# Folding the next batch on GpSimd, row copies on VectorE, and other steps for the transforms

## The chip, the cores and the metric

One Trainium2 chip, one of its cores. The metric is the device time of one execution in microseconds (us). The engines are named as the trace names them: PE is TensorE (matmuls; PEld its weight loads), DVE is VectorE, ACT is ScalarE, POOL is GpSimd, SP is the engine that issues most DMAs.

## The reference

```python
X = np.fft.fft(x, axis=1)                 # x: 8 batches, 3072 positions, 256 features
X = np.fft.fft(X, axis=2).real            # 24576 tokens of 256
h = x @ w_in                              # 256 -> 2048
g = h * (1.0 / (1.0 + np.exp(-1.702 * h)))
x = g @ w_out                             # 2048 -> 256
# second MoE layer: tokens with x @ w_skip > 0 go to the expert of the largest gate logit
y[mask] = gate_w[mask, None] * (np.maximum(xc[mask] @ w1[e], 0.0) @ w2[e])
out[do_compute] = xc + y
```

All of it is in float32. The kernel gets that accuracy from matmuls with operands split into a high and a low part (`yh`, `yl`, `gh`, `gl`, `sh`, `sl`, `woh`, `wol`): the low part is the value minus its rounded high part.

## The kernel before

Phase 1 makes the Fourier transform and the first MLP and routes tokens to experts; phase 2 runs the eight experts over the routed rows. The change touches phase 1 alone.

The transform over the sequence is cut by symmetry. **Folds** first add and subtract mirrored rows of a batch, which arrive as six `raw` tiles: `pq` (512 columns), `eo` (two of 256), `ub` (two of 128), `va` (two of 128; for the middle pair of tiles, t = 1, four of 64 partitions), and once for each pair of tiles `tm` (256 and twice 128). ACT rounds `tm` and `va` to `sh`, POOL subtracts to get `sl`. Each batch then has eight **transforms** (`piece_mm`: 9 matmuls into the one PSUM bank with the tag "misc"), four even and four odd, whose results DVE, ACT and POOL turn into `yh` and `yl`.

Phase 1 then walks over 16 half-batches `hb` of 24 steps, 384 steps `g` in all. A block `gb` is 512 tokens and 8 steps; the 2048 hidden units are taken 256 a step. In step g:

- `hstep(g)`: 12 matmuls (L850) to two `pt` tiles (three PSUM buffers), then on DVE `pp` twice (L854) and `h` twice (L856, L857);
- `ystep(g - 2)`: 24 matmuls (L881) from `gh` and `gl` of two steps before into four PSUM banks y0 to y3. In a block's last step the order is bank by bank, in the others all `gh` parts come ahead of all `gl` parts;
- `gelu(g)`: ACT makes `gh` (L864) and `h` (L865), POOL makes `gl = h - gh` (L866). `h` and `gl` have two buffers, `gh` three;
- two steps after a block's last step `finish` copies the four banks to `rows` (L887: y0, y1 on DVE, y2, y3 on ACT). The next `ystep` starts a new block in these banks and needs them free;
- last, the **side list** of the step: functions that `plan` has put there by step number (transforms, their evacuations, folds, loads), and the route that `finish` appends. A block that is copied in step n (n = 1, 9, 17 of a half-batch, from the block before) has `a1` in step n + 1 (on DVE: the row ids at L891, then `route1`, six small operations L779 to L784 that end in `roh`, and the store of the rows), `a2` in n + 2 (PE: small matmuls of `roh`, L793 and L795, into the "misc" bank), `a3` in n + 3 (DVE, L805 to L809), and one scatter (POOL, an indirect DMA, L813) in each of n + 4 to n + 7.

Every engine takes its instructions in the order in which the program emits them; waits between engines are semaphores. So the step numbers in `plan` decide what stands ahead of what. Odd transforms of a batch run in its even half-batch, even transforms of the next batch in its odd one. The folds of the next batch also begin in the even half-batch and reach into the odd one (steps 24 and up are steps 0 and up of the odd one). The folds of batch 1, in half-batch 0, have a list of slots of their own.

Of the kernel before, what the change touches and what calls it, by code (L numbers as in the profile page):

```python
# [18 lines left out]
ALU = mybir.AluOpType  # L19
# [15 lines left out]
TB = 512  # L35
NBLK = HC // PB
NSTEP = NF // 2
RW = 266
NW = 264
# [125 lines left out]
class Phase1:  # L165
# [53 lines left out]
        e2.tensor_sub(eo[:, 1], pq[:, 0], pq[:, 1])  # L219
        return eo  # L220

    def fold_ub(self, ab, eo, ub):
        v = self.nc.vector
        v.tensor_add(ub[:, 0, ab], eo[:, 0, 0], eo[:, 0, 1])
        v.tensor_sub(ub[:, 1, ab], eo[:, 1, 0], eo[:, 1, 1])

    def fold_va(self, t, ab, eo, va):
        v = self.nc.vector
        for kind, op in ((0, v.tensor_sub), (1, v.tensor_add)):
            x, y = eo[:, kind, 0], eo[:, kind, 1]  # L230
            at_a = ab == kind
            if t == 1:
                if at_a:
                    op(va[0:64, kind, 0, 1], x[0:64], y[0:64])
                    op(va[64:128, kind, 1, 1], x[64:128], y[64:128])
                else:
                    op(va[64:128, kind, 0, 1], x[0:64], y[0:64])
                    op(va[0:64, kind, 1, 1], x[64:128], y[64:128])
            else:
                op(va[:, kind, t // 2, 0 if at_a else 2], x, y)  # L240

    def fold_tm(self, ub):
        v = self.nc.vector
        tm = self.fb.tile([P, 4, P], F32, tag="tm", bufs=1, name="tm")
        v.tensor_add(tm[:, 0::3], ub[:, :, 0], ub[:, :, 1])
        v.tensor_sub(tm[:, 2], ub[:, 0, 0], ub[:, 0, 1])
        v.tensor_sub(tm[:, 1], ub[:, 1, 0], ub[:, 1, 1])
        return tm

    def fold_even(self, t, ub, sh, sl, le):  # L250
        tm = self.fold_tm(ub)
        shv, slv = sh[:, :, t], sl[:, :, t]
        self.nc.scalar.copy(shv, tm)
        le.tensor_sub(slv, tm, shv)
# [83 lines left out]
    def startup(self):  # L338
# [156 lines left out]
        def fold(j):  # L495
            if j % 2 == 0:
                q["ub"] = self.new_ub()
            eo = q["eo", j] = st.tile([P, 2, 2, P], F32, name=f"eo{j}")
            self.fold_ub(j % 2, self.fold_eo(self.fold_pq(raws[j], v), v, eo), q["ub"])

        def tmsh(t):
            q["tm"] = self.fold_tm(q["ub"])
            act.copy(sh[:, :, t], q["tm"])

        def slv(t):
# [136 lines left out]
                if (n or k == "c") and (n < 9 or k == "a"):  # L642
                    at(n, k, f, n)
        for j in range(6):
            at(j + 1, "d", lambda j=j: self.fold_va(j // 2, j % 2, q.pop(("eo", j)), va))
        at(3, "c", self.ahead_pad)
        for f, fe, p, n in ((piece, piece_ev, 2, 1), (piece, piece_ev, 3, 1), (nine, nine_ev, 2, 3), (nine, nine_ev, 4, 5), (nine, nine_ev, 5, 6)):
            at(n, "d", f, p)
# [7 lines left out]
    def plan(self, hb):  # L656
        nc = self.nc
        b, odd = hb // 2, hb % 2
        g0 = hb * NBLK * NSTEP
        last = hb == 2 * self.nb - 1  # L660
        if last:
            return
        add = lambda s, f: self.side[g0 + s].append(f)
        le = nc.gpsimd
        st = {}
        if not odd:
            def prep():
                st["cm"] = self.cm if hb == 0 else self.cmn
                st["y"] = self.new_y(hb + 1)
                self.y[hb + 1] = st["y"]  # L670
            add(9 if hb == 0 else 0, prep)
            if hb == 0:
                for c in range(4):
                    add(7 + c, lambda c=c: self.split_odd(self.va, *self.s, c, le))
            def p0(p):
                sh, sl = self.s
                q = self.piece_mm(st["cm"][4 + p % 2], sh, sl, p, KC)
                st["q"] = q
            def e0(p):
                st["xp"] = self.evac_odd0(b, p, st["q"])  # L680
            def e1(p):
                self.evac_odd1(p, st["xp"], st["q"], *st["y"], le)
            for p, s in enumerate((10, 13, 15, 21) if hb == 0 else (1, 4, 6, 7)):
                add(s, lambda p=p: p0(p))
                add(s + 1, (lambda p=p: e0(p)) if p % 2 == 0 else (lambda p=p: e1(p)))
            if b + 1 < self.nb:
                def ld(i):
                    st["r", i] = self.load_raw(b + 1, i // 2, i % 2)

                def f1(i):  # L690
                    st["pq"] = self.fold_pq(st["r", i], nc.vector)
                    if i + 3 < 6:
                        ld(i + 3)

                def f2(i):
                    if i == 0:
                        self.va = self.new_va()
                    if i % 2 == 0:
                        st["ub"] = self.new_ub()
                    st["eo"] = self.fold_eo(st["pq"], nc.vector)  # L700

                def fa(i):
                    f1(i)
                    f2(i)

                def fu(i):
                    self.fold_ub(i % 2, st["eo"], st["ub"])

                def fv(i):
                    self.fold_va(i // 2, i % 2, st["eo"], self.va)  # L710

                def fr(i):
                    fu(i)
                    fv(i)

                def fe(t):
                    if t == 0:
                        self.sn = self.new_s()
                    self.fold_even(t, st["ub"], *self.sn, le)

                def nx():
                    self.s = self.sn
                    self.cmn = {0: self.load_c(0), 1: self.load_c(1)}

                if hb == 0:
                    seq = []
                    for t in range(3):
                        for i in (2 * t, 2 * t + 1):
                            seq += [lambda i=i: fa(i), lambda i=i: fr(i)]
                        seq.append(lambda t=t: fe(t))  # L730
                    slots = (13, 15, 19, 21, 23, 24, 27, 29, 30, 31, 32, 35, 37, 38, 39)
                    for i in range(3):
                        add(10 + i, lambda i=i: ld(i))
                    for s, f in zip(slots, seq):
                        add(s, f)
                else:
                    for i in range(3):
                        add(i, lambda i=i: ld(i))
                    for f, steps in ((f1, (3, 11, 14, 21, 24, 29)), (f2, (6, 13, 16, 21, 24, 29)), (fu, (6, 13, 16, 23, 27, 30)), (fv, (7, 14, 19, 22, 27, 30)), (fe, (15, 23, 31))):
                        for i, s in enumerate(steps):  # L740
                            add(s, lambda f=f, i=i: f(i))
                add(23, nx)
        else:
            def prep():
                st["cm"] = self.cmn
                st["y"] = self.new_y(hb + 1)
                self.y[hb + 1] = st["y"]
            add(0, prep)
            def p0(p):
                sh, sl = self.s  # L750
                st["q"] = self.piece_mm(st["cm"][p], sh, sl, p, CW if p == 0 else KC)
                if p < 2:
                    st["cm"][p + 2] = self.load_c(p + 2)
                else:
                    self.cmn2 = getattr(self, "cmn2", {}) if p == 3 else {}
                    self.cmn2[p + 2] = self.load_c(p + 2)
                    if p == 3:
                        self.cmn = self.cmn2
            def e0(p):
                self.evac_even(b + 1, p, st["q"], *st["y"], le)  # L760
            for p, s in enumerate((16, 18, 20, 22) if b == 0 else (10, 13, 15, 18)):
                add(s, lambda p=p: p0(p))
                add(s + 1, lambda p=p: e0(p))
            def sp(c):
                if c == 0:
                    self.s = self.new_s()
                self.split_odd(self.va, *self.s, c, le)
            for c in range(4):
                add(22 + c // 2 if b == 0 else 20 + c, lambda c=c: sp(c))
# [57 lines left out]
    def main(self):  # L827
# [10 lines left out]
        if True:  # L838
# [44 lines left out]
            def finish(gb, gnow):  # L883
                st = {}
                rows = self.rp.tile([P, 4, RW], F32, tag="rows", bufs=2, name="rows")
                for t in range(4):
                    (v.tensor_copy if t < 2 else nc.scalar.copy)(rows[:, t, :NW], ys[gb][t])  # L887
                del ys[gb]

                def a1():  # L890
                    v.scalar_tensor_tensor(rows[:, :, NW:], self.rid[:, 1], float(gb * TB), self.rid[:, 0], ALU.mult, ALU.add)  # L891
                    st["oh"] = self.route1(rows, 4)
                    nc.sync.dma_start(self.a["out"][gb * TB : (gb + 1) * TB].rearrange("(t p) d -> p t d", p=P), rows[:, :, :D])

# [505 lines left out]
```

## Time and profile before

| | us |
|---|---|
| median of 3 runs | 2405.22 (2400.37 to 2409.26) |
| the profiled execution | 2406.35 |
| its span, first to last instruction | 2404.2 |
| PE busy in the span | 2344.2 (98%) |
| DVE busy | 1682.4 (70%) |
| ACT busy | 1121.3 (47%) |
| POOL busy | 1396.3 (58%) |

The profiled execution lies 1.1 us above the median of the runs. Ends of matmuls are modelled, and a matmul is recorded for longer than the next one's distance from it, so a busy PE does not say that no time is lost: for that one compares how long steps take that hold the same work. The start of a step is the first L850 matmul of its `hstep`. A window cut from one such start to the next gives the length of a step.

### The profile page before, as it was taken

The page shows a single profiled execution, that of the slowest core. Times are in us where ns is not written, and L with a number is a line of the kernel's source. Part 1 is how long each engine was busy: PE and PEld are TensorE (multiplying, and loading weights), DVE is VectorE, ACT ScalarE, POOL GpSimd, SP SyncE. Part 2 cuts the span into 40 slices and gives each one's busy share as a digit, 9 for nine tenths or more (in the row PEclk, how much of TensorE's full clock was granted, in tenths as well). Part 3 has the DMA queues.
Part 4 walks back from the last instruction along what each step waited for, and adds up shares of the span by engine and source line. Part 5 has one row for each costly group of instructions (what it writes and reads, how often), then busy time and mean ns, then how long its engine had stood idle before and what let it go on. Part 6 is the DMA issues. An engine that isn't in the chain of part 4 may idle for free. (4 is left out here: it accounts for less than half of the span.)

```text
span 2404.2 us, 50497 instructions
## 1 busy us (share of the span) xinstructions
PE 2344.2 (98%) x19222; PEld 2308.6 (96%) x19222; DVE 1682.4 (70%) x3429; ACT 1121.3 (47%) x1451; POOL 1396.3 (58%) x868
## 2 busy tenths in 40 slices
PE   6999999999999999999999999999999999999999
PEld 4899999999999999999999999999999999999999
DVE  7679679768966896698679768965756445555543
ACT  5644545455454454455444455445544333433332
POOL 3567667676677676767767767667666312323211
PEclk8999999999999999999999999999999999999999
DMA  7312312231131123112312221130101312323111
GB/s 261 117 34 78 125 44 69 66 102 37 66 99 63 46 70 113 47 38 85 116 34 79 73 87 48 60 105 21 62 20 33 108 44 84 116 84 119 36 45 39
DMA packets 91449, 178.82 MB, mean 74 GB/s; under 512 B 10895, under 2 KB 66750, under 8 KB 85104
## 3 DMA queue, kind: packets, MB, share of 16 engines
q1 hardware_dynamic: 69488, 96.12, 12.9%
q0 software_dynamic: 20448, 77.87, 9.3%
q8 instruction: 132, 2.16, 0.4%
q10 hardware_dynamic: 1312, 2.10, 0.3%
q14 instruction: 69, 0.57, 0.1%
HBM read 126.21 MB, written 66.59 MB: 80 GB/s over the span
## 5 line engine op out<-in xcount | busy, mean ns | idle before, releaser
L866 POOL TENSOR_TENSOR gl<-h,gh 128x1024 fp32r<-128x1024 f32 x384 | 922.7, 2403 | 519.0 <-ACT h L865 429.4
L864 ACT ACTIVATE gh<-h 128x1024 fp32r<-128x1024 f32 x384 | 407.5, 1061 | 854.4 <-DVE h L857 711.7
L881 PE MATMUL py<-woh,gh 128*128 128x264 f32 x3072 | 771.0, 285 | 9.6 <-ACT rows L887 9.0
L881 PE MATMUL py<-wol,gh 128*128 128x264 f32 x3072 | 767.0, 283 | 0.0
L881 PEld LDWEIGHTS py<-woh,gh 128*128 128x128 f32 x3072 | 579.4, 189 | 14.2 <-ACT rows L887 13.6
L881 PEld LDWEIGHTS py<-wol,gh 128*128 128x128 f32 x3072 | 578.5, 188 | 0.0
L854 DVE SCALAR_TENSOR_TENSOR pp<-rb,w,pt 128x256 f32<-128x256 f32 x768 | 333.6, 475 | 297.1 <-PE pt L850 296.6
L881 PE MATMUL py<-woh,gl 128*128 128x264 f32 x3072 | 460.8, 284 | 0.9 <-POOL gl L866 0.9
L850 PE MATMUL pt<-yh,wch 128*128 128x256 f32 x1536 | 434.1, 283 | 4.4 <-DVE pp L854 2.8
L850 PE MATMUL pt<-yl,wch 128*128 128x256 f32 x1536 | 429.2, 279 | 0.5 <-POOL yl L300 0.5
L850 PE MATMUL pt<-yh,wcl 128*128 128x256 f32 x1536 | 428.5, 279 | 0.0
L865 ACT ACTIVATE h<-h 128x1024 f32<-128x1024 f32 x384 | 407.6, 1061 | 36.2 <-ACT gh L864 1.5
L881 PEld LDWEIGHTS py<-woh,gl 128*128 128x128 f32 x3072 | 410.0, 189 | 1.1 <-POOL gl L866 1.1
L856 DVE TENSOR_TENSOR h<-pp,pt 128x512 f32<-128x512 f32 x384 | 264.4, 689 | 55.9 <-POOL gl L866 4.6
L850 PEld LDWEIGHTS pt<-yh,wch 128*128 128x128 f32 x1536 | 290.5, 189 | 5.7 <-DVE pp L854 3.3
L850 PEld LDWEIGHTS pt<-yl,wch 128*128 128x128 f32 x1536 | 291.7, 190 | 1.0 <-POOL yl L300 0.7
L850 PEld LDWEIGHTS pt<-yh,wcl 128*128 128x128 f32 x1536 | 290.6, 189 | 0.0
L1281 POOL DMA_INDIRECT out<-ob,ix x82 | 80.3, 980 | 337.3 <-DVE ob L1295 335.1
L857 DVE TENSOR_TENSOR h<-pp,pt 128x512 f32<-128x512 f32 x384 | 261.3, 680 | 0.0
L813 POOL DMA_INDIRECT xs<-rows,rix x192 | 194.7, 1014 | 44.1 <-issue 25.0
L1267 PE MATMUL h<-xh,w1h 128*128 128x256 f32 x656 | 184.4, 281 | 5.6 <-PEq L1325 3.8
L1303 PE MATMUL po<-w2h,hh 128*128 128x256 f32 x656 | 188.6, 287 | 0.0
(221 smaller groups left out, 3493.9 us busy)
## 6 DMA issues: line engine op xcount, KB each, us to landing
cmat<-cm POOLq DMA_DIRECT2D x48, 1158.0 KB
raw<-raw SPq DMA_DIRECT2D x48, 512.0 KB
out<-rows SPq DMA_DIRECT2D x48, 512.0 KB
r<-w SPq DMA_DIRECT2D x14, 1024.0 KB
nx<-xs SPq DMA_DIRECT2D x33, 266.0 KB, 3.0
rb<-yd SPq DMA_DIRECT2D x48, 128.0 KB
wide<-w_in SPq DMA_DIRECT2D x8, 512.0 KB
wide<-w_out SPq DMA_DIRECT2D x8, 512.0 KB
```

The costliest lines, as they stand in the source:

```text
L813: i = self.nc.gpsimd.indirect_dma_start(self.xs, bass.IndirectOffsetOnAxis(ap=ix[:, t : t + 1], axis=0), rows[:, t], None, bounds_check=E ...
L850: nc.tensor.matmul(pt[z][:, i], lhsT=w_[:, z, f], rhs=x_[:, z, cols], start=n == 0, stop=n == 2)
L854: v.scalar_tensor_tensor(pp[:, i], r, self.w128[:, 2 * s + i : 2 * s + i + 1], pt[0][:, i], ALU.mult, ALU.add)
L856: v.tensor_add(h[:, :, 0], pp, pt[1])
L857: v.tensor_sub(h[:, :, 1], pp, pt[1])
L864: nc.scalar.activation(gh, hv, AF.Gelu_apprx_sigmoid)
L865: nc.scalar.activation(hv, hv, AF.Gelu_apprx_sigmoid)
L866: nc.gpsimd.tensor_sub(gl, hv, gh)
L881: nc.tensor.matmul(ys[gb][t], lhsT=x_[:, i, tk], rhs=w_[:, 2 * s + i], start=s == 0 and part is hi and n == 0, stop=ends and part is lo an ...
L1267: nc.tensor.matmul(h[:, z], lhsT=w_[:, k, f * P : (f + 1) * P], rhs=x_[:, k], start=i == 0, stop=i == 5)
L1281: d = self.nc.gpsimd.indirect_dma_start(self.out, bass.IndirectOffsetOnAxis(ap=ix, axis=0), ob, None, bounds_check=self.ntok - 1, oob_is_e ...
L1303: self.nc.tensor.matmul(po[t], lhsT=x_[:, f, t * P : (t + 1) * P], rhs=w_[:, f], start=f == 0 and n == 0, stop=f == 7 and n == 2)
```

## The change

1. The folds that start in the even half-batches 2 to 12 (six of the seven times that a next batch is folded inside the loop) run on POOL: `fold_pq`, `fold_eo`, `fold_ub`, `fold_tm` and `fold_va`, this one without t = 1, which stays on DVE. Half-batch 0 keeps its folds on DVE and its slots.
2. `fold_even` is split in `ft` (the `tm` fold) and `fc` (the copy on ACT and the subtraction on POOL), with steps of their own; all fold steps are new, and the first three raw loads are issued three steps earlier.
3. The row ids are written on POOL in `finish`: a memset of one column and an add, in place of one operation on DVE in `a1`.
4. All four row copies are on DVE.
5. Transforms: odd ones from steps 1, 4, 6, 7 to 1, 5, 7, 13; even ones from 10, 13, 15, 18 to 8, 13, 15, 17. Half-batches 0 and 1 keep theirs.

```diff
-            for p, s in enumerate((10, 13, 15, 21) if hb == 0 else (1, 4, 6, 7)):
+            for p, s in enumerate((10, 13, 15, 21) if hb == 0 else (1, 5, 7, 13)):
...
+                fo = nc.vector if hb == 0 else nc.gpsimd
...
-                    st["pq"] = self.fold_pq(st["r", i], nc.vector)
+                    st["pq"] = self.fold_pq(st["r", i], fo)
...
-                    st["eo"] = self.fold_eo(st["pq"], nc.vector)
+                    st["eo"] = self.fold_eo(st["pq"], fo)
...
-                    self.fold_ub(i % 2, st["eo"], st["ub"])
+                    self.fold_ub(i % 2, st["eo"], st["ub"], fo)
...
-                    self.fold_va(i // 2, i % 2, st["eo"], self.va)
+                    self.fold_va(i // 2, i % 2, st["eo"], self.va, nc.vector if i // 2 == 1 else fo)
...
-                def fe(t):
+                def ft(t):
+                    st["tm"] = self.fold_tm(st["ub"], fo)
+
+                def fc(t):
                     if t == 0:
                         self.sn = self.new_s()
-                    self.fold_even(t, st["ub"], *self.sn, le)
+                    self.split_even(t, st["tm"], *self.sn, le)
...
-                        add(i, lambda i=i: ld(i))
-                    for f, steps in ((f1, (3, 11, 14, 21, 24, 29)), (f2, (6, 13, 16, 21, 24, 29)), (fu, (6, 13, 16, 23, 27, 30)), (fv, (7, 14, 19, 22, 27, 30)), (fe, (15, 23, 31))):
+                        add(i - 3, lambda i=i: ld(i))
+                    for f, steps in ((f1, (1, 4, 9, 16, 22, 26)), (f2, (2, 5, 11, 17, 24, 27)), (fu, (3, 7, 12, 18, 25, 28)), (fv, (3, 8, 13, 19, 25, 28)), (ft, (10, 20, 29)), (fc, (15, 21, 30))):
...
-            for p, s in enumerate((16, 18, 20, 22) if b == 0 else (10, 13, 15, 18)):
+            for p, s in enumerate((16, 18, 20, 22) if b == 0 else (8, 13, 15, 17)):
...
+                nc.gpsimd.memset(rows[:, :, NW : NW + 1], 0.0)
+                nc.gpsimd.tensor_scalar_add(rows[:, :, RW - 1 :], self.rid[:, 0, :, 1:], float(gb * TB))
                 for t in range(4):
-                    (v.tensor_copy if t < 2 else nc.scalar.copy)(rows[:, t, :NW], ys[gb][t])
+                    v.tensor_copy(rows[:, t, :NW], ys[gb][t])
...
-                    v.scalar_tensor_tensor(rows[:, :, NW:], self.rid[:, 1], float(gb * TB), self.rid[:, 0], ALU.mult, ALU.add)
```

What this makes of the order on two engines, for half-batch 2. On DVE, from the `h` of step 17 to the first route operations of step 18, the order before was:

```order
L856 TENSOR_TENSOR h<-pp,pt 128x2x256
L857 TENSOR_TENSOR h<-pp,pt 128x2x256
L887 COPY rows<-py_4163 128x264
L887 COPY rows<-py_4164 128x264
L854 SCALAR_TENSOR_TENSOR pp<-rb,w_71,pt 128x256 x2
L856 TENSOR_TENSOR h<-pp,pt 128x2x256
L857 TENSOR_TENSOR h<-pp,pt 128x2x256
L891 SCALAR_TENSOR_TENSOR rows<-rid 128x4x2
L779 TENSOR_REDUCE rm<-rows 128x4
L780 TENSOR_TENSOR rq<-rows,rm 128x32
```

Now (the lines of the changed kernel are some five higher):

```order
L861 TENSOR_TENSOR h<-pp,pt 128x2x256
L862 TENSOR_TENSOR h<-pp,pt 128x2x256
L894 COPY rows<-py_4171 128x264
L894 COPY rows<-py_4172 128x264
L894 COPY rows<-py_4173 128x264
L894 COPY rows<-py_4174 128x264
L859 SCALAR_TENSOR_TENSOR pp<-rb,w_71,pt 128x256 x2
L861 TENSOR_TENSOR h<-pp,pt 128x2x256
L862 TENSOR_TENSOR h<-pp,pt 128x2x256
L784 TENSOR_REDUCE rm<-rows 128x4
L785 TENSOR_TENSOR rq<-rows,rm 128x32
```

Two copies came from ACT, and the row ids are gone from the head of the route.

On POOL, from step 22 of half-batch 2 to the scatter of step 24, the order before was (`xs` is a scatter, `cmat` a load of transform matrices, `sl` the low part of folded rows):

```order
L866 TENSOR_TENSOR gl<-h,gh 128x1024
L813 DMA xs<-rows,rix 198720x266
L866 TENSOR_TENSOR gl<-h,gh 128x1024
L254 TENSOR_TENSOR sl<-tm,sh 128x4x128
L202 DMA cmat_4964<-cm 128x2316
L202 DMA cmat_4966<-cm 128x2316
L813 DMA xs<-rows,rix 198720x266
L866 TENSOR_TENSOR gl<-h,gh 128x1024
L813 DMA xs<-rows,rix 198720x266
```

Now, for the same three steps:

```order
L871 TENSOR_TENSOR gl<-h,gh 128x1024
L212 TENSOR_TENSOR pq<-raw_2_0_3839 128x512
L818 DMA xs<-rows,rix 198720x266
L871 TENSOR_TENSOR gl<-h,gh 128x1024
L202 DMA cmat_4974<-cm 128x2316
L202 DMA cmat_4976<-cm 128x2316
L818 DMA xs<-rows,rix 198720x266
L871 TENSOR_TENSOR gl<-h,gh 128x1024
L218 TENSOR_TENSOR eo<-pq 128x256
L219 TENSOR_TENSOR eo<-pq 128x256
L818 DMA xs<-rows,rix 198720x266
```

A fold now stands between one `gl` and the next, behind the `gl` of its own step and ahead of that step's scatter; `sl` moved to step 21.

## Rows read from the trace of the kernel before

**Rows 1.** The page: busy time of each engine in the span.

```profile
PE 2344.2 (98%) x19222; PEld 2308.6 (96%) x19222; DVE 1682.4 (70%) x3429; ACT 1121.3 (47%) x1451; POOL 1396.3 (58%) x868
```

**Rows 2.** Windows, half-batches 4, 5, 14: length, busy of PE, PEld, DVE, ACT, POOL.

```profile
519.26:630.00 110.74, 110.15 (x918) 109.79 (x917) 90.25 (x178) 54.05 (x59) 75.91 (x41) 1.00 0.13 43
630.00:742.36 112.36, 111.37 (x917) 110.74 (x916) 83.17 (x165) 57.21 (x64) 81.12 (x50) 1.00 0.30 98
...
1635.51:1745.60 110.09, 109.92 (x917) 109.57 (x916) 70.53 (x144) 54.41 (x58) 75.23 (x41) 1.00 0.14 45
```

**Rows 3.** Windows of single steps: plain; with transform; with `a2`; step 18 of half-batch 14.

```profile
560.20:564.47 4.27, 4.27 (x37) 4.27 (x37) 3.09 (x6) 0.99 (x1) 3.08 (x2) 1.00 0.04 14
548.45:554.29 5.84, 5.84 (x47) 5.84 (x46) 4.82 (x6) 4.24 (x5) 4.27 (x2) 1.00 0.00 0
724.91:729.32 4.41, 4.41 (x41) 4.41 (x39) 3.19 (x9) 2.95 (x4) 2.72 (x2) 1.00 0.36 142
1719.74:1724.02 4.28, 4.28 (x39) 4.28 (x37) 3.15 (x6) 2.71 (x5) 3.80 (x3) 1.00 0.41 138
```

**Rows 4.** Sums over six step windows each: even 18; odd 2, 11, 18, 19.

```profile
sum 30.97, PE 27.41 PEld 26.17 DVE 29.82 ACT 25.78 POOL 26.72; mean PE 4.57 PEld 4.36 DVE 4.97 ACT 4.30 POOL 4.45
...
sum 31.39, PE 27.36 PEld 26.11 DVE 27.56 ACT 23.07 POOL 30.10; mean PE 4.56 PEld 4.35 DVE 4.59 ACT 3.85 POOL 5.02
...
sum 30.27, PE 27.42 PEld 26.78 DVE 27.34 ACT 4.15 POOL 15.18; mean PE 4.57 PEld 4.46 DVE 4.56 ACT 0.69 POOL 2.53
...
sum 37.53, PE 37.15 PEld 35.89 DVE 33.85 ACT 28.73 POOL 21.48; mean PE 6.19 PEld 5.98 DVE 5.64 ACT 4.79 POOL 3.58
...
sum 28.91, PE 27.34 PEld 26.64 DVE 26.83 ACT 3.67 POOL 13.15; mean PE 4.56 PEld 4.44 DVE 4.47 ACT 0.61 POOL 2.19
```

**Rows 5.** PE's waits, half-batches 2 to 13: total, times, longest.

```profile
PE py L881 <- ACT rows L887: 7.6, 12, 0.8
PE pmisc L793 <- DVE xt L278: 4.4, 11, 1.0
```

**Rows 6.** Timeline, half-batch 4, step 18: start, duration, instruction, wait ahead.

```profile
605.85 0.64 ACT L887 COPY rows<-py 128x264 f32<-128x264 f32 x2
...
606.27 0.39 PE L881 MATMUL py<-woh,gh 128*128 128x264 f32 x1 [0.59 <-ACT rows L887]
```

**Rows 7.** Groups by line and engine: count, busy us, mean ns, idle ahead.

```profile
L866 POOL TENSOR_TENSOR gl<-h,gh 128x1024 fp32r<-128x1024 f32 x384 | 922.7, 2403 | 519.0 <-ACT h L865 429.4 <-PE pt L850 60.8 <-ACT gm L978 8.2
L813 POOL DMA_INDIRECT xs<-rows,rix x192 | 194.7, 1014 | 44.1 <-issue 25.0 <-DVE cnt L1138 8.3 <-PE py L881 3.1
...
L335 POOL TENSOR_TENSOR wol<-cv,woh 128x512 fp32r<-128x512 f32 x8 | 10.3, 1286 | 33.0 <-ACT woh L334 33.0
...
L527 POOL TENSOR_TENSOR s9a<-raw 128x96 f32<-128x96 f32 x1 | 0.8, 757 | 3.8 <-DMA raw<-raw 3.8
...
L887 DVE COPY rows<-py 128x264 f32<-128x264 f32 x96 | 36.9, 425 | 0.9 <-PE py L881 0.9
```

**Rows 8.** Timeline, half-batch 4, steps 8 to 10: POOL, then PE's `gl` matmuls.

```profile
565.78 2.40 POOL L866 TENSOR_TENSOR gl<-h,gh 128x1024 fp32r<-128x1024 f32 x1 [2.35 <-ACT h L865]
568.13 1.86 POOL L300 TENSOR_TENSOR yl<-xt,yh 128x768 fp32r<-128x768 f32 x1
570.15 0.99 POOL L813 DMA_INDIRECT xs<-rows,rix  x1 [0.15 <-issue]
571.17 2.42 POOL L866 TENSOR_TENSOR gl<-h,gh 128x1024 fp32r<-128x1024 f32 x1
...
566.33 0.41 PE L881 MATMUL py<-woh,gl 128*128 128x264 f32 x2
...
572.06 1.14 PE L881 MATMUL py<-woh,gl 128*128 128x264 f32 x8
```

**Rows 9.** Timeline, half-batch 4: `gl` and a route operation; `pp` of step 11.

```profile
608.85 2.40 POOL L866 TENSOR_TENSOR gl<-h,gh 128x1024 fp32r<-128x1024 f32 x1 [0.42 <-ACT h L865]
...
609.01 2.28 DVE L781 SCALAR_TENSOR_TENSOR rq<-rq,k 128x32 f32<-128x32 f32 x1
...
576.82 0.47 DVE L854 SCALAR_TENSOR_TENSOR pp<-rb,w,pt 128x256 f32<-128x256 f32 x1
```

More of the change, by code (lines that the diff above doesn't have):

```diff
@@ L220, in fold_eo, with fold_ub, fold_va @@
         return eo
-    def fold_ub(self, ab, eo, ub):
-        v = self.nc.vector
+    def fold_ub(self, ab, eo, ub, v):
         v.tensor_add(ub[:, 0, ab], eo[:, 0, 0], eo[:, 0, 1])
         v.tensor_sub(ub[:, 1, ab], eo[:, 1, 0], eo[:, 1, 1])
-    def fold_va(self, t, ab, eo, va):
-        v = self.nc.vector
+    def fold_va(self, t, ab, eo, va, v):
         for kind, op in ((0, v.tensor_sub), (1, v.tensor_add)):
@@ L240, in fold_va, with fold_tm @@
                 op(va[:, kind, t // 2, 0 if at_a else 2], x, y)
-    def fold_tm(self, ub):
-        v = self.nc.vector
+    def fold_tm(self, ub, v):
         tm = self.fb.tile([P, 4, P], F32, tag="tm", bufs=1, name="tm")
@@ L248, in fold_tm, with split_even @@
         return tm
-    def fold_even(self, t, ub, sh, sl, le):
-        tm = self.fold_tm(ub)
+    def split_even(self, t, tm, sh, sl, le):
         shv, slv = sh[:, :, t], sl[:, :, t]
@@ L498, in fold @@
             eo = q["eo", j] = st.tile([P, 2, 2, P], F32, name=f"eo{j}")
-            self.fold_ub(j % 2, self.fold_eo(self.fold_pq(raws[j], v), v, eo), q["ub"])
+            self.fold_ub(j % 2, self.fold_eo(self.fold_pq(raws[j], v), v, eo), q["ub"], v)
         def tmsh(t):
-            q["tm"] = self.fold_tm(q["ub"])
+            q["tm"] = self.fold_tm(q["ub"], v)
             act.copy(sh[:, :, t], q["tm"])
@@ L644, in startup @@
         for j in range(6):
-            at(j + 1, "d", lambda j=j: self.fold_va(j // 2, j % 2, q.pop(("eo", j)), va))
+            at(j + 1, "d", lambda j=j: self.fold_va(j // 2, j % 2, q.pop(("eo", j)), va, v))
         at(3, "c", self.ahead_pad)
@@ L714, in fr, with fe @@
                     fv(i)
-                def fe(t):
+                def ft(t):
+                    st["tm"] = self.fold_tm(st["ub"], fo)
+                def fc(t):
                     if t == 0:
                         self.sn = self.new_s()
-                    self.fold_even(t, st["ub"], *self.sn, le)
+                    self.split_even(t, st["tm"], *self.sn, le)
+                def fe(t):
+                    ft(t)
+                    fc(t)
                 def nx():
```

## The prediction

> **What bounds the kernel now.** I read the page first: PE is busy 98% of the span, DVE 70%, POOL 58% [rows 1]. That share can't show what a change of order is worth, so I went to lengths of steps. A plain step takes 4.27 us, one with a transform 5.84, one with the small route matmuls of `a2` 4.41 [rows 3]; these repeat to 0.01, so PE's own work sets them, and every step that holds the same work and takes longer has lost time. In half-batches 2 to 13 five places lose time in every pair of half-batches [rows 4], six times each:
>
> - step 18 of the even one: 30.97 - 6 x 4.28 = 5.3 us;
> - step 2 of the odd one: 31.39 - 6 x 4.28 = 5.7;
> - odd step 11 (holds `a2`): 30.27 - 6 x 4.41 = 3.8;
> - odd step 18 (holds a transform): 37.53 - 6 x 5.84 = 2.5;
> - odd step 19 (holds `a2`): 28.91 - 6 x 4.41 = 2.5.
>
> Together 19.8 us. The list of PE's waits names two causes [rows 5]. Twelve times PE waited for a row copy on ACT: steps even 18 and odd 2. Eleven times `a2` waited for the `xt` of a transform evacuated in the same step, because both use the "misc" bank: odd 11 and odd 19. The waits add to 12.0 us where the lengths give 17.3; ends of matmuls are modelled, so the lengths are what I use. Odd step 18 has no wait named; as a step after a row copy it looks like the first kind.
>
> Why is the ACT copy late? In the timeline PE stands until the ACT copies run at 605.85 [rows 6]; in ACT's order they come behind the `gelu` of the same step, which waits for DVE's `h`, and DVE is behind with folds. Half-batch 14 tests that: no folds there, copies still on ACT, DVE busy 70.5 in place of 90.3 us [rows 2], and its step 18 takes 4.28 [rows 3].
>
> **The change, part by part.** I sum against the profiled execution's own 2406.35 us.
>
> *Row copies on DVE: what it removes.* The fourth copy waits for the bank that is finished last, at the end of the step; at 0.43 us each [rows 7] they end about 0.6 into the next step, ahead of that step's `pp` (about 0.9 in: the first two matmul groups have to be there) and of the first use of bank y0 after 12 matmuls. So the copies hide in a gap of DVE, provided that DVE is on time. Without the folds it is, as half-batch 14 shows. I take back 5.3 + 5.7 + 2.5 = 13.5 us.
>
> *Transforms moved.* Even transforms at 8, 13, 15, 17 free the bank at 9, 14, 16, 18; `a2` stands at 11 and 19, so no evacuation is ahead of it in its step. 3.8 + 2.5 = 6.3 us. The matrix loads that each transform issues move with it on POOL's queue; the shortest lead (13 to 17) is 4 steps, two of them with transforms, some 20 us. The raw loads go earlier on SP and a later raw load waits there for a fold on POOL; only stores of rows and loads some steps ahead of their use stand behind it. I cost both at nothing.
>
> *Folds on POOL.* The cost is from POOL's own rows. 1024 columns take 2403 ns, 512 take 1286 [rows 7], so a column is 2.18 ns and the fixed part 170. Queued operations overlap by 0.05 (a `gl` at 565.78 of 2.40, the next operation at 568.13) and a scatter costs 1.18 from the end of the operation ahead to the `gl` behind it (569.99 to 571.17) [rows 8]. So `gl` 2.35, `pq` 1.24, `eo` 1.36, `ub` 0.80, `va` 0.80, `tm` 1.48, a 512-column `sl` 1.24, `yl` 1.82 as shown. A batch moves 6 x (1.24 + 1.36 + 0.80) + 4 x 0.80 + 3 x 1.48 = 28 us; the row ids, two tiny operations with no close row, I put at 0.3 a block. A pair of half-batches has 223 us and POOL is busy 157 of it [rows 2]: room on average. But the folds lie unevenly. Going through the new step numbers, POOL's work in steps 14 to 31 is 5.4, 4.8, 4.8, 4.0, 3.2, 2.4, 3.8, 4.8, 4.8, 4.6, 4.9, 4.3, 3.6, 3.7, 4.0, 5.0, 4.8, 3.5: 76.1 us (the two matrix loads of step 23 counted as one scatter). The 18 steps take 77.3. So POOL is full for 18 steps and the question is how late `gl` gets.
>
> An undelayed `gl` starts 5.58 into its step (565.78 with the step's start at 560.20). It ends at 568.18 and PE first uses it at 572.06 [rows 8]: it may start 3.88 later, at 9.46. In a block's last step PE wants it 1.45 earlier (the first `gl` matmul 1.86 after the step's start at 564.47, against 3.31), so up to 8.01. Adding work and subtracting steps from 5.58 at step 14 (step 13 holds a transform and lets POOL catch up): 6.7, 7.2, 7.7, 7.4 at steps 15 to 18. The route of step 18 then waits for POOL (next paragraph) and makes `h` of step 19 late, so `gl` starts at 8.1 and 7.4 in steps 19 and 20; then 6.9, 7.4, 7.9 (step 23, a block's last), 8.2, 8.9, 8.8, 8.2, 7.5, 7.1, 7.8, 8.3. The worst margins are 0.1 us in step 23 and 0.6 in step 25. In step 31, a block's last too, the transform now in step 32 gives 1.57 more. The ledger just closes.
>
> *The lock.* A DVE operation with two inputs in SBUF and a POOL operation exclude each other here: L781 was issued at 609.01 and ended at 611.29, 0.04 after the `gl` that ran from 608.85 [rows 9]. Four such operations are in `a1` (L780, L781, L783, L784; L891, the fifth, goes). Before, the route of step 10 ended so late that `pp` of step 11 started at 576.82, 3.8 into its step [rows 9], without loss; the second half of `hstep` needs that `pp` (0.87 for both) about 0.7 into the next step, so 4.27 + 0.7 - 0.87 = 4.1 is the limit. After it, each of the four lets one POOL operation pass. In step 10 these are `gl`, the ids, `pq` and the next `gl`, whose end at about 8.2 puts `pp` at 3.9; in step 18 `gl`, the ids and two `eo`, 3.4; in step 26 `gl`, the ids and two `ub`, about 4. All are near the limit and none is over it.
>
> The Trainium skill (Perfetto Trace Analysis, Optimizing Scalar/DVE Operations) warns that moving work between these two engines may not help, since GpSimd's only SBUF port is the second one of VectorE and is held as an exclusive lock. The lock is in this trace; by the rule the time would stay near 2406, and that is the second rival.
>
> *Sum.* 2406.35 - 13.5 - 6.3 = 2386.6. For margins of 0.1 to 0.6 us with estimated durations I charge 0.8 us a batch, 4.8 in all: 2391.4. The row copies in half-batch 1 and the 1.4 us that a route loses without L891 I leave out.
>
> **Rivals.**
>
> 1. *POOL's small operations are dearer than my line says; slower.* The one small operation among the rows, 96 columns, took 757 ns [rows 7] where the line gives 380. Steps 14 to 31 hold 29 moved operations; 0.38 more for each is 11 us, of which 1.2 are spare; POOL is full, so the rest becomes PE waiting for `gl`: 6 x 9.8 = 59, 2387 + 59 = 2446. It ends slower than before by 0.5% from 0.22 us an operation on. Against it: that row is a first operation that follows a DMA, and the 384- to 1024-column rows lie on one line.
>
> 2. *The lock gives it back; the same.* If `gl` of step 9, 17 or 25 is 1 us later than I have it, the four route operations meet one more `gl` and `pp` comes at 5 to 6 in place of 4: 1 us in each of three steps of a batch, 18 us: 2386.6 + 18 = 2405. For it: my three values are all within 0.7 of the limit. Against it: before, the same route lost nothing with `pp` at 3.8.
>
> 3. *Only the transforms' part comes.* If row copies on DVE are as late as those on ACT were, because `a1` or `a3` keeps DVE behind: 2406 - 6.3 = 2400.
>
> 4. *More comes.* A pair of half-batches without any loss would be 48 x 4.27 + 8 x 1.57 + 6 x 0.14 = 218.4 against 223.1, 28 us in all: 2378.
>
> **Numbers.** A change of 0.5% (12 us) is about what a measurement of this kernel can tell from none. Forecast 2391, own range 2385 to 2396: 0.50. Rival 1: 0.13; rival 2: 0.25; rival 3: 0.07; rival 4: 0.05. Faster by over 0.5% (below 2393.2 from the median 2405.2) holds most of the forecast and rival 4: 0.53; the same 0.34; slower 0.13. The range from 2380 to 2412 takes in the bounds of the forecast and of rivals 2 and 3, and leaves out rival 1 and the far end of rival 4.
>
> **What would show it.** Right: even step 18 and odd step 2 at 4.28, odd 11 and 19 at 4.41; no wait for a row copy; POOL's fold groups at 1.2 to 1.3 (512 columns), 0.7 (256), 0.4 to 0.5 (128); no `a2` waiting for `xt`. Wrong: `gl` in the list of PE's waits in steps 23 to 28 (rival 1); `pp` or `roh` there, in steps 11, 19 and 27 (rival 2).

## The result, and the profile after

The changed kernel takes 2421.94 us (2420.39 to 2425.57, 5 runs) against 2405.22: ratio 1.0077 [1.0058, 1.0095]. It is slower by 0.8%, where 2391 us was forecast. The profiled span is 2422.5 us (2404.2 before). Ratios, here and below, are estimated from all runs but one slow one of e5 (3822 us), so they can differ by 0.1% from the quotient of the medians.

First the page's busy times, the line that answers to [rows 1]:

```profile
PE 2349.9 (97%) x19222; PEld 2320.0 (96%) x19222; DVE 1532.4 (63%) x3195; ACT 1095.8 (45%) x1355; POOL 1579.1 (65%) x1246
```

150 us went from DVE and 183 came to POOL, as planned (28 us a batch and 0.3 a block make 182). Now the five places of [rows 4], in the same order (even 18; odd 2, 11, 18, 19), and two new ones, even 19 and even 20; each line sums six step windows:

```profile
sum 25.69, PE 25.69 PEld 25.69 DVE 15.54 ACT 12.69 POOL 24.64; mean PE 4.28 PEld 4.28 DVE 2.59 ACT 2.12 POOL 4.11
...
sum 25.95, PE 25.95 PEld 25.95 DVE 15.74 ACT 13.08 POOL 24.74; mean PE 4.33 PEld 4.33 DVE 2.62 ACT 2.18 POOL 4.12
...
sum 28.15, PE 27.04 PEld 26.55 DVE 24.13 ACT 9.81 POOL 23.02; mean PE 4.51 PEld 4.42 DVE 4.02 ACT 1.63 POOL 3.84
...
sum 25.62, PE 25.62 PEld 25.62 DVE 18.98 ACT 10.56 POOL 19.30; mean PE 4.27 PEld 4.27 DVE 3.16 ACT 1.76 POOL 3.22
...
sum 26.52, PE 26.52 PEld 26.23 DVE 16.19 ACT 15.51 POOL 18.86; mean PE 4.42 PEld 4.37 DVE 2.70 ACT 2.59 POOL 3.14
...
sum 44.08, PE 27.34 PEld 26.65 DVE 28.09 ACT 6.75 POOL 41.86; mean PE 4.56 PEld 4.44 DVE 4.68 ACT 1.13 POOL 6.98
...
sum 35.53, PE 35.53 PEld 35.53 DVE 33.21 ACT 14.41 POOL 10.34; mean PE 5.92 PEld 5.92 DVE 5.54 ACT 2.40 POOL 1.72
```

The forecast gains are there: against the plain lengths, five places that lost 19.8 us now lose 2.0, nearly all in odd step 11. But even step 19 (holds `a2`, should be 4.41) takes 7.35 on average and step 20 (should be 4.35) 5.92: 17.6 + 9.4 = 27 us lost. Steps 3 and 4 of half-batch 13, once, cost 6.9 more. So 17.8 us were regained and 33.9 lost, in all 16.1 of the 18.3 us by which the spans differ.

In the list of PE's waits for half-batches 2 to 13 the two causes of [rows 5] are gone, and one is new:

```profile
PE pmisc L798 <- DVE roh L789: 24.2, 11, 4.3
```

`roh` is the route's result, for which `a2` waits. Why it is late is seen in half-batch 4, whose step 18 starts at 609.18, step 19 at 613.47. Here is the timeline of POOL, then of DVE, then of PE:

```profile
611.02 1.29 POOL L212 TENSOR_TENSOR pq<-raw 128x512 f32<-128x512 f32 x1
612.47 0.99 POOL L818 DMA_INDIRECT xs<-rows,rix  x1 [0.16 <-DVE h L862]
613.47 2.44 POOL L871 TENSOR_TENSOR gl<-h,gh 128x1024 fp32r<-128x1024 f32 x1
615.80 0.15 POOL L891 MEMSET rows<- 128x4 f32 x1
616.04 0.23 POOL L892 TENSOR_SCALAR rows<-rid 128x4 f32<-128x4 f32 x1
616.35 0.73 POOL L218 TENSOR_TENSOR eo<-pq 128x256 f32<-128x256 f32 x1
617.04 0.73 POOL L219 TENSOR_TENSOR eo<-pq 128x256 f32<-128x256 f32 x1
617.73 2.34 POOL L871 TENSOR_TENSOR gl<-h,gh 128x1024 fp32r<-128x1024 f32 x1
...
615.98 0.19 DVE L784 TENSOR_REDUCE rm<-rows 128x4 f32<-128x32 f32 x1 [3.61 <-POOL rows L891]
...
617.39 0.40 DVE L788 SCALAR_TENSOR_TENSOR rm<-rows,rm 128x4 f32<-128x4 f32 x1
617.82 2.29 DVE L789 TENSOR_TENSOR roh<-rq,rm 128x32 bf16<-128x32 f32 x1
620.04 0.86 DVE L859 SCALAR_TENSOR_TENSOR pp<-rb,w,pt 128x256 f32<-128x256 f32 x2
...
620.17 0.18 PE L798 MATMUL pmisc<-roh,tri 128*128 128x32 bf16 x1 [2.27 <-DVE roh L789]
```

DVE is free at 612.37, but the route's first operation reads the eighth logit, the zero column, and that is now written by POOL's memset, queued behind a `gl` that starts only at 613.47. DVE stands 3.61 us. Then the route meets `eo`, `eo` and the next `gl`, and `pp` of step 19 starts 6.57 into its step, where the limit was 4.1. In half-batches 6 to 12 a second thing comes on top: one route operation (L786) waits through `gl` and `ub`, 3.3 us, and `pp` starts 7.3 to 7.4 into the step.

### The profile page after: what moved, and what is told of

Its sections match the earlier page's. It is cut to its first block, busy times and chain, and to the rows that moved or that the text cites. A ratio compares the mean times of both kernels' runs of the same rounds, so it can differ in the third digit from the quotient of the medians.

```text
span 2422.5 us, 50479 instructions
## 1 busy us (share of the span) xinstructions
PE 2349.9 (97%) x19222; PEld 2320.0 (96%) x19222; DVE 1532.4 (63%) x3195; ACT 1095.8 (45%) x1355; POOL 1579.1 (65%) x1246
## 5 line engine op out<-in xcount | busy, mean ns | idle before, releaser
L871 POOL TENSOR_TENSOR gl<-h,gh 128x1024 fp32r<-128x1024 f32 x384 | 923.8, 2406 | 352.2 <-ACT h L870 313.3
L886 PE MATMUL py<-wol,gh 128*128 128x264 f32 x3072 | 775.6, 286 | 0.0
L886 PEld LDWEIGHTS py<-woh,gh 128*128 128x128 f32 x3072 | 587.9, 191 | 1.1 <-issue 0.8
L886 PEld LDWEIGHTS py<-wol,gh 128*128 128x128 f32 x3072 | 586.6, 191 | 0.0
L1273 PE MATMUL h<-xl,w1h 128*128 128x256 f32 x656 | 185.1, 282 | 2.3 <-issue 2.2
```

The source lines that it names most:

```text
L871: nc.gpsimd.tensor_sub(gl, hv, gh)
L886: nc.tensor.matmul(ys[gb][t], lhsT=x_[:, i, tk], rhs=w_[:, 2 * s + i], start=s == 0 and part is hi and n == 0, stop=ends and part is lo an ...
L1273: nc.tensor.matmul(h[:, z], lhsT=w_[:, k, f * P : (f + 1) * P], rhs=x_[:, k], start=i == 0, stop=i == 5)
```

## The experiments

Labels e1 to e14; ratios are to the kernel before on the same chip. Even 19 or odd 3 means the sum of six windows, 26.5 when nothing is lost.

**e1.** The zero column on VectorE.

```
-                nc.gpsimd.memset(rows[:, :, NW : NW + 1], 0.0)
+                v.memset(rows[:, :, NW : NW + 1], 0.0)
```

> The zero column of a block's rows is written by VectorE, ahead of its four row copies, in place of GpSimd; the row ids and all else as in the changed kernel. Theory (the route's first operation waits for the zero column, which stands behind a gl on GpSimd): the 3.6 us that DVE stands before L784 in even step 18 go, pp of even step 19 starts at most 4.3 into its step in place of 6.6, even step 19 takes about 4.4 in place of 7.5 and step 20 about 4.35 in place of 5.9 in all six batches, and odd step 3 of half-batch 13 (8.85) falls below 5: 2421.9 - 6 x 4.3 = 2396, with half-batch 13 too 2389 to 2397. Rival (the lock: the four two-input operations of the route meet gl, eo, eo and the next gl in any case): pp of step 19 still more than 5.5 into its step, 2415 to 2422.

Measured: 2409.66, ratio 1.0010 [1.0001, 1.0019]. Of the 0.77% that the change lost, 0.67% (16 us) is this one write. But it is not the 2389 to 2397 that the theory gave: even 19 fell to 35.31 only, and odd step 3 of half-batch 13 stayed at 8.84 (there L785, a route operation, waited 8.28). Timeline of half-batch 6, whose step 19 runs from 825.35 to 831.97:

```profile
824.39 2.91 DVE L785 TENSOR_TENSOR rq<-rows,rm 128x32 f32<-128x32 f32 x1
...
828.25 3.10 DVE L788 SCALAR_TENSOR_TENSOR rm<-rows,rm 128x4 f32<-128x4 f32 x1
...
827.87 0.73 POOL L219 TENSOR_TENSOR eo<-pq 128x256 f32<-128x256 f32 x1
828.57 2.35 POOL L871 TENSOR_TENSOR gl<-h,gh 128x1024 fp32r<-128x1024 f32 x1
830.89 0.44 POOL L223 TENSOR_TENSOR ub<-eo 128x128 f32<-128x128 f32 x1
```

L788 has two inputs in SBUF and takes 0.16 us where nothing holds it up. It is issued during `eo`, and by the prediction's count it should go next. A **hand-over** is the moment when the GpSimd operation that holds the lock ends: L788 loses the one after `eo` to the `gl` queued there, and the next one to `ub`. In half-batch 4 of the same run the same operation took 0.57 and nothing was lost. So both theories hold a part: the wait for the zero column, and the lock.

**e2.** Zero column and ids on GpSimd, issued ahead of that step's `gl`.

```
+                if done and (g - LAG) % NSTEP == NSTEP - 1:
...
+                    nc.gpsimd.memset(rows[:, :, NW : NW + 1], 0.0)
...
                 if g < total:
                     gelu(g)
```

> Zero column and row ids stay on GpSimd, but are issued ahead of the gl of the same step in place of behind it. Theory (place in GpSimd's order, not the engine): like the kernel with the zero column on VectorE, within 5 us of it, 2390 to 2400; even step 19 below 4.9. Rival (GpSimd is full in these steps, so any operation ahead of gl only shifts the wait, or the lock decides): 2415 to 2422, even step 19 still above 6.5.

Measured: 2417.74, 1.0044 [1.0029, 1.0059]. The time is the rival's, but not all of its picture came: half-batches 4 and 2 are nearly cured (step 19 at 4.51 and 4.64), the four others still have step 19 at 7.4, where L788 again lost to `gl` and `ub` (3.1 us). The place in the queue matters, but does not save the time.

**e3.** Ids and zero in one VectorE operation in `a1`, as before.

```
-                nc.gpsimd.memset(rows[:, :, NW : NW + 1], 0.0)
-                nc.gpsimd.tensor_scalar_add(rows[:, :, RW - 1 :], self.rid[:, 0, :, 1:], float(gb * TB))
...
+                    v.scalar_tensor_tensor(rows[:, :, NW:], self.rid[:, 1], float(gb * TB), self.rid[:, 0], ALU.mult, ALU.add)
                     st["oh"] = self.route1(rows, 4)
```

> Row ids and zero column go back to one VectorE operation at the head of the route, with two inputs in SBUF, as in the kernel before; folds, transforms and row copies as in the changed kernel. Theory (what costs is the wait for a write that is queued on GpSimd): nothing of the route waits for that queue, 2390 to 2400, even step 19 below 5.4. Rival (lock alone): five two-input operations meet one GpSimd operation more than four do, pp of step 19 6 us or more into its step, even step 19 above 6.5, 2415 to 2425.

Measured: 2451.85, 1.0189 [1.0173, 1.0204]: worse than the change, even 19 at 40.70 and odd 3 at 53.31. The rival won, and by more than it said. One VectorE operation of half-batch 5, step 2, and POOL beside it:

```profile
655.20 8.34 DVE L786 SCALAR_TENSOR_TENSOR rq<-rq,k 128x32 f32<-128x32 f32 x1
...
654.87 1.03 POOL L818 DMA_INDIRECT xs<-rows,rix  x1 [0.18 <-DVE rows L896]
655.91 2.41 POOL L871 TENSOR_TENSOR gl<-h,gh 128x1024 fp32r<-128x1024 f32 x1
658.27 0.47 POOL L223 TENSOR_TENSOR ub<-eo 128x128 f32<-128x128 f32 x1
658.69 0.46 POOL L224 TENSOR_TENSOR ub<-eo 128x128 f32<-128x128 f32 x1
659.11 0.86 POOL L238 TENSOR_TENSOR va<-eo 128x128 f32<-128x128 f32 x2
659.94 2.33 POOL L871 TENSOR_TENSOR gl<-h,gh 128x1024 fp32r<-128x1024 f32 x1
662.24 1.25 POOL L212 TENSOR_TENSOR pq<-raw 128x512 f32<-128x512 f32 x1
```

0.19 us of work waited through the end of a scatter and seven queued operations; it ended when nothing more was queued on POOL.

**e4.** The fourth `eo` a step later: `(f2, (2, 5, 11, 17, 24, 27))` becomes `(f2, (2, 5, 11, 18, 24, 27))`.

> The changed kernel with the fourth fold's eo (two operations of 0.73) one step later, in step 18 in place of 17, so that it stands behind the gl that it stood ahead of; the zero column stays on GpSimd behind gl. If the wait for the zero column alone makes the route late (start at 2.5 into step 19 in any case), and the eo pair with the next gl adds nothing, even step 19 stays above 6.5: 2415 to 2422. If wait and lock add up (2.5 us by the zero column, then eo, eo and gl passed one for each two-input operation, 0.5 + 0.2 + 2.1), then without the eo pair between, the route ends about 617.0 in place of 620.0 in half-batch 4, pp of step 19 is 3.5 into its step, and steps 19 and 20 are back at 4.4 to 4.6: about 2396 to 2402, with half-batch 13 as it is.

Measured: 2424.36, 1.0077 [1.0061, 1.0092], no change. In half-batch 4 the `eo` pair left, but `gl` moved up into its place and L786 waited 2.34 for that instead; `pp` of step 19 starts no earlier (6.74 into it).

**e5.** The kernel before with row copies on VectorE and the new transform steps, nothing else.

```
-                    (v.tensor_copy if t < 2 else nc.scalar.copy)(rows[:, t, :NW], ys[gb][t])
+                    v.tensor_copy(rows[:, t, :NW], ys[gb][t])
...
-            for p, s in enumerate((16, 18, 20, 22) if b == 0 else (10, 13, 15, 18)):
+            for p, s in enumerate((16, 18, 20, 22) if b == 0 else (8, 13, 15, 17)):
```

> The kernel before with two parts of the change alone: the four row copies on VectorE, and the transforms at their new steps; folds and row ids as before. Theory (the forecast's sum, 13.5 + 6.3, was right, and what was lost came with the folds on GpSimd): steps even 18 and odd 2 at 4.28, odd 11 and 19 at 4.41, 2407.7 - 19.8 = 2388 (2384 to 2394). Rival (with the folds still on it VectorE is as late for the copies as ScalarE was, so the copies' part does not come): 2400 to 2404.

Measured: 2415.5, 1.0032 [1.0022, 1.0043], slower than both theories gave. Odd 11 and 19 came (26.57, 26.49), but even 18 rose to 49.75: with the folds still on it, DVE reaches the row copies far too late. Half-batch 6, step 18 from 832.83:

```profile
828.18 2.74 DVE L218 TENSOR_TENSOR eo<-pq 128x256 f32<-128x256 f32 x1
830.84 0.41 DVE L219 TENSOR_TENSOR eo<-pq 128x256 f32<-128x256 f32 x1
831.18 3.18 DVE L224 TENSOR_TENSOR ub<-eo 128x128 f32<-128x128 f32 x1
...
836.68 1.44 DVE L887 COPY rows<-py 128x264 f32<-128x264 f32 x4
```

The folds themselves have two inputs in SBUF and wait for POOL: L218 and L224 take 2.74 and 3.18, where L219 and L225 behind them take 0.41 and 0.28.

**e6.** Run e1 with half of the folds (the last three of six) back on VectorE, away from the steps of row copy and route. `va` of the third fold goes to GpSimd with the rest of it.

```
+                fold = lambda i: fo if i < 3 else nc.vector
...
-                    for f, steps in ((f1, (1, 4, 9, 16, 22, 26)), (f2, (2, 5, 11, 17, 24, 27)), (fu, (3, 7, 12, 18, 25, 28)), (fv, (3, 8, 13, 19, 25, 28)), (ft, (10, 20, 29)), (fc, (15, 21, 30))):
+                    for f, steps in ((f1, (1, 4, 9, 19, 22, 26)), (f2, (2, 5, 11, 20, 24, 27)), (fu, (3, 7, 12, 20, 25, 28)), (fv, (3, 8, 13, 21, 25, 28)), (ft, (10, 21, 29)), (fc, (15, 22, 30))):
```

> The kernel of the first experiment (zero column on VectorE) with the last three of a batch's six folds back on VectorE, at steps 19 to 30, and the first three on GpSimd at steps 1 to 13; GpSimd is then full in no stretch. Theory (a VectorE operation with two inputs in SBUF waits behind several queued GpSimd operations only where GpSimd's queue is full, steps 16 to 28): even step 19 at 4.41 in all six, odd step 3 of half-batch 13 too, no wait of a2 for roh above 1 us in half-batches 2 to 13, 2383 to 2392. Rival (the route loses to GpSimd whatever stands there, or VectorE is late with its folds): even step 19 or odd 3 above 5.5 in some, 2398 to 2410.

Measured: 2390.94, 0.9930 [0.9915, 0.9945]: faster than both kernels. Even 19 is at 26.80, odd 3 at 26.49. Half-batches 4 and 5, for [rows 2]:

```profile
519.98:629.83 109.85, 109.85 (x917) 109.70 (x916) 72.41 (x163) 53.79 (x54) 93.12 (x71) 1.00 0.12 40
629.83:740.03 110.20, 110.20 (x917) 110.00 (x916) 74.98 (x165) 54.30 (x57) 80.71 (x51) 1.00 0.31 103
```

The pair takes 220.05 where it took 223.1. Half-batch 2 still loses 7 us, 4 of them in step 22. Fewer folds on GpSimd and other steps for the rest came together here; which of the two did it is not shown.

**e7, e8.** The kernel of e5 with unused operations on GpSimd behind the `gl` of each block's last step: six of 128 columns, or two of 512.

```
+                    for i in range(6):
+                        nc.gpsimd.tensor_add(self.dum[:, :128], z, z)
```

> The kernel of run e5 with six added GpSimd operations of 128 columns (0.42 each, 2.5 us in all, their result unused) behind the gl of each block's last step in half-batches 2 to 13, 36 trains in all, just where the route stands; nothing waits for them by data. If each of the route's two-input operations lets one GpSimd operation pass (what the forecast assumed), the route is through after gl and three of the six, no step gets longer, and the time is that of e5 within 4 us; no route operation lasts over 2.6 us. If a waiting VectorE operation can lose to a whole train, single route operations last 3 us and more in some of the 36, pp of the next step starts over 4.1 into it, and the time is 5 to 40 us above e5.

> As e7 with two operations of 512 columns (1.24 each, 2.5 us in all) in place of six of 128. By the forecast's count (one GpSimd operation for each two-input operation) the route meets gl, both added ones and the next gl, and ends 8.7 us after the start of its step, 0.3 late in each of 36 places: some 10 us above e5 and above e7. If what counts is the number of hand-overs that VectorE can lose, it is at most as slow as e7.

Measured: e7 2421.35, 1.0064 [1.0047, 1.0081], 6 us above e5; e8 2470.73, 1.0264 [1.0247, 1.0281], 55 above. In e7 no route operation took longer than 2.3 us. But in e5 DVE is late for reasons of its own, and the added operations read one broadcast column, so e10 and e11 repeat both on e6.

**e9.** Run e6 with the memset back on GpSimd (the diff of e1 reversed).

> Run e6 (first three folds on GpSimd, last three on VectorE) with the zero column back on GpSimd behind gl, as in the change. Theory (that wait costs only where GpSimd is full and gl therefore late; where gl runs on time it ends about when h is done, and the route's second operation would wait for it anyway): within 4 us of e6, even step 19 at 4.4. Rival (the place behind gl costs by itself): even step 19 above 5 and 8 us or more above e6.

Measured: 2431.54, 1.0099 [1.0083, 1.0114], 40 us above e6. My theory fell: the zero column costs even more where GpSimd is not full. By the trace it starts small, and early, in step 10. The route and `pp` of step 11 in half-batch 4 of e9, whose step 10 starts at 573.70 and step 11 at 578.04:

```profile
577.52 0.18 DVE L786 TENSOR_REDUCE rm<-rows 128x4 f32<-128x32 f32 x1 [0.62 <-POOL rows L893]
577.74 0.19 DVE L787 TENSOR_TENSOR rq<-rows,rm 128x32 f32<-128x32 f32 x1
577.97 1.25 DVE L788 SCALAR_TENSOR_TENSOR rq<-rq,k 128x32 f32<-128x32 f32 x1
...
579.48 2.21 DVE L790 SCALAR_TENSOR_TENSOR rm<-rows,rm 128x4 f32<-128x4 f32 x1
...
582.33 0.86 DVE L861 SCALAR_TENSOR_TENSOR pp<-rb,w,pt 128x256 f32<-128x256 f32 x2
```

A wait of 0.62 puts the route behind `pq` and then the next `gl`: `pp` comes 4.29 into step 11, in e6 (573.41 with step 11 from 572.15) 1.26. `gl` of step 11 then starts 9.0 into its step and not 5.9, and what follows, the folds on DVE included, runs late: step 22 sums to 43.19 over the six. That the late `gl` of step 11 makes step 22 long is argued, no run tests it alone; but e6 has the same in one place: in half-batch 2, where `gl` of step 11 starts at 9.1, step 22 takes 8.29, in its other five 4.27.

**e10, e11.** Run e6 with six operations of 128 columns, or two of 512, that read two different inputs.

```
+                        nc.gpsimd.tensor_add(self.dum, self.wch[:, 0, f], self.wch[:, 1, f])
```

> Run e6 with six added GpSimd operations of 128 columns with two different inputs (about 0.45 each, result unused) behind the gl of each block's last step in half-batches 2 to 13, 36 trains; in e6 VectorE comes to the route on time, which in e7 it did not, and e7's added operations read one broadcast column. If each two-input operation of the route lets one GpSimd operation pass: through after gl and three of the six, within 5 us of e6, no route operation over 2.6 us. If a waiting operation can lose to a whole train: some route operations last over 3 us, pp of the next step starts over 4.1 into it, 8 to 60 us above e6.

> As e10 with two operations of 512 columns (1.3 each) in place of six of 128. By the count of one for one the route meets gl, both, and the next gl: pp of the next step 0.3 past its limit in 36 places, 10 us above e6, and above e10. If VectorE can lose a whole train, e10 and e11 cost about the same, since both trains end at the same time.

Measured: e10 2394.75, 0.9950 [0.9935, 0.9965], 4 above e6; e11 2492.22, 1.0355 [1.0340, 1.0371], 101 above. Nearly the same POOL time (2.8 and 2.6 us a place) cost 4 us in short pieces and 101 in long ones. VectorE mostly got in between the short ones (by the count in the last section 11 times of 14), and no operation lost twice. In e11, in half-batch 7, a `pq` on VectorE and three route operations met `gl`, both long ones and the next `gl`, and `pp` came 7.4 into step 3. The direction was that of the one-for-one count; its size (10) was wrong tenfold, since `pp` lands not 0.3 but 2 to 3.3 us past its limit where `gl` is not at its earliest.

**e12.** Run e6, the fourth `ub` and `va` a step later: `fu` at 21 and `fv` at 22.

> Run e6 with the fourth fold's ub and va one step later (21 and 22 in place of 20 and 21), so that eo and ub of one fold on VectorE no longer stand ahead of one step's pp. Theory (step 22 of half-batch 2, 8.29 in e6, came from eo and ub waiting for two gl in a row): that step at 4.3, some 4 us below e6, 2384 to 2391. Rival (which operation meets which gl only shifts to another place): within 3 us of e6, or a long step elsewhere in half-batch 2.

Measured: 2390.71, 0.9933 [0.9920, 0.9947], as e6. The pair of half-batches 4 and 5 is now 219.58, but the loss of half-batch 2 only moved on into the first step of half-batch 3 (9.90): the rival.

**e13, e14.** The changed kernel with the zero column on VectorE for the route of even step 10 alone, and for all but that one.

```
+                (v if gnow % (2 * per) == NSTEP + 1 else nc.gpsimd).memset(rows[:, :, NW : NW + 1], 0.0)
```

> The changed kernel with the zero column on VectorE only for the blocks whose route stands in even step 10 (one block in six; the others on GpSimd as in the change). Theory (the loss begins in step 10: 0.7 us of wait there make the route meet pq, gl and tm, pp of step 11 comes at 4.3 in place of 1.25, gl of step 11 starts at 9.0 in place of 5.9, and GpSimd, full from step 14 on, is late until step 19): gl of step 11 at 5.9, of step 17 at 7.8, and the time is that of run e1 within 4 us, 2406 to 2414. Rival (the wait of 3.6 us in step 18 itself, which this kernel keeps, makes the loss): even steps 19 and 20 still lose 4 us, 2417 to 2422.

> The opposite: the zero column on VectorE for all blocks but those whose route stands in even step 10. Theory (it begins in step 10): gl of step 11 still at 9.0 and of step 17 at 8.5, even step 19 still above 6.5 in nearly all six, 2416 to 2422. Rival (the wait of step 18 itself): steps 19 and 20 near 4.4, 2396 to 2411.

Measured: e13 2420.04, 1.0066 [1.0053, 1.0080]; e14 2405.57, 0.9999 [0.9990, 1.0009]. The theory that the loss begins in step 10 fell. In e13 `gl` is early again (5.9 in step 11, 7.8 in step 17), and even 19 is still long; in e14 it is cured. The first line is e13, the second e14:

```profile
sum 40.56, PE 27.33 PEld 26.64 DVE 28.15 ACT 6.88 POOL 38.33; mean PE 4.56 PEld 4.44 DVE 4.69 ACT 1.15 POOL 6.39
...
sum 26.50, PE 26.50 PEld 26.20 DVE 25.50 ACT 6.77 POOL 26.15; mean PE 4.42 PEld 4.37 DVE 4.25 ACT 1.13 POOL 4.36
```

So in the changed kernel it is step 18's own wait that costs. But e1, which differs from e14 in the route of step 10 alone, has even 19 at 35.31: what happens in step 10 moves things in step 18 too, and e14's full cure is in part luck. Its time is not clearly better than that of e1 (the intervals overlap), for it loses elsewhere, in odd step 1, to waits for `gl`. PE's waits in the whole of e14:

```profile
PE py L886 <- POOL gl L871: 7.0, 7, 1.3
```

## Why the prediction was wrong

**What held.** The two gains were read rightly: even 18, odd 2 and odd 18 gave back 5.3 + 5.4 + 2.5 of the 13.5, odd 11 and 19 gave 4.5 of the 6.3 and the rest in e12 (odd 11 at 26.51). e6, with half of the folds moved and the zero column left on VectorE, is 0.7% below the kernel before, about the forecast's net gain (15 of 2406), though with another set of folds. The condition "provided that DVE is on time" was needed, as e5 shows. POOL's prices held: one operation of 512, 256, 128 columns takes 1.30, 0.74, 0.47 us, in the groups of the changed kernel:

```profile
L212 POOL TENSOR_TENSOR pq<-raw 128x512 f32<-128x512 f32 x36 | 46.6, 1295 | 0.3
...
L219 POOL TENSOR_TENSOR eo<-pq 128x256 f32<-128x256 f32 x36 | 26.6, 739 | 0.0
...
L223 POOL TENSOR_TENSOR ub<-eo 128x128 f32<-128x128 f32 x36 | 16.9, 470 | 0.1
...
L892 POOL TENSOR_SCALAR rows<-rid 128x4 f32<-128x4 f32 x48 | 11.7, 243 | 2.3
L891 POOL MEMSET rows<- 128x4 f32 x48 | 5.6, 116 | 0.2 <-DMA xs<-rows,rix 0.2
```

So rival 1's price is out. The ledger of `gl` held too where nothing else disturbed it (its 18 terms add to 76.4, not 76.1, so 0.9 us was spare and not 1.2): in half-batch 4 of e1 `gl` starts 6.7, 7.2, 7.8, 7.7, 8.1, 7.6 into steps 15 to 20, against 6.7, 7.2, 7.7, 7.4, 8.1, 7.4; by step 25 it was 0.8 too low. It did not quite close: in e14 `gl` of step 23 starts 9.0 to 9.4 into its step, where the ledger has 7.9 with a margin of 0.1, PE waits 0.9 to 1.3 us for it in all six batches, and odd step 1 loses 7.8 us, where 4.8 were charged. In the changed kernel this does not show, since the wait in step 19 gives GpSimd time to catch up (`gl` of step 21 starts 5.9 into its step).

**The first step that failed: the row ids "at 0.3 a block".** Their cost is right (0.24 + 0.12), their dependency was not followed. The removed VectorE operation (L891 of the kernel before) wrote not only the ids but the zero column, on the engine that reads it; after the change the route waits across engines, behind a whole `gl`. That is 16 us here (e1; 19 by e14), 40 in the lighter kernel (e9).

**The second: "each of the four lets one POOL operation pass".** That gave `pp` at 3.4 in step 19. In e1 it is 3.5 in half-batch 4 and 6.4 in the later ones: VectorE does not always get the next turn. Where it loses, one `gl` more is passed. The other 19 us, from e1 to e6, go when POOL's queue is thinned and the folds leave the steps of the route: 12 of them in even steps 19 and 20, 6 in steps 3 and 4 of half-batch 13. This is what rival 2 feared, one `gl` more in the step after a route, but not by its condition: `gl` of step 17 was not 1 us late in e1 (7.8 where the ledger has 7.7), the hand-over was lost. I gave it 0.25, and priced it at 1 us a place where it was 2.2 to 4.4. The changed kernel is 17 us over rival 2's 2405; the first step's 16 are about that.

**The third: a wait of PE was priced as its own length.** After it PE's granted clock fell to its lower level, which no term held. Windows of steps 19 and 20 of half-batch 4, the granted clock being the number ahead of the last two:

```profile
613.47:620.29 6.82, 4.55 (x43) 4.44 (x42) 4.13 (x7) 1.12 (x2) 6.66 (x7) 1.00 0.02 8
620.29:626.21 5.92, 5.92 (x41) 5.92 (x39) 5.53 (x15) 2.40 (x3) 2.12 (x3) 0.71 0.00 0
```

Step 20 has no wait and costs 1.57 us more: 9.4 us in six batches.

What stays open is which hand-overs VectorE loses: mostly the same ones in the batches of one run, and others after small shifts of `gl`.

## What to carry to other kernels

When a small write moves to another engine, follow who reads it, and what stands ahead of the write in its new queue: a 0.1 us memset cost 16 to 40 us. Ahead of a chain of short VectorE operations with two SBUF inputs, count the long GpSimd operations that it can meet, not GpSimd's load, and keep those steps free of moved work. If each part of a change is worth something only with another (row copies here only with folds away from VectorE), try the smallest set together before all of it.

## What the runs showed of the hardware

- A waiting VectorE operation mostly gets the next turn at the lock, but not surely. I counted the route's operations with two SBUF inputs in half-batches 2 to 13 that had been issued at least 0.1 us before a GpSimd operation ended with the next one already queued (scatters left out). 43 of 49 went first in the changed kernel, 23 of 35 in e1, 29 of 46 in e3. One that had lost usually lost the next hand-over too (8 of 12, 14 of 22, 41 of 48), and stood up to 8.34 us. The Trainium skill (SBUF — State Buffer, SBUF: two separate sides) says that whichever starts first holds the pair for the whole instruction and the other fully blocks; the trace agrees, and shows that a blocked operation can stay blocked over several.
- After the 2.27 us wait in half-batch 4 TensorE's clock was at its lower level (0.50 of full, 1.2 GHz) for 3.41 us, from 621.67. In e1 the four waits of 2.06 to 2.07 in step 19 were followed by such a fall in two half-batches (step 20 at 5.93) and by none in two (4.41, 4.37).
